# Scores of 27 tiles of the last batch are computed in the first 28 steps and kept in DRAM, and the first batch's last 64 queries become parts of their own

## The chip, the cores and the metric

The kernel runs on one core of one Trainium2 chip. The metric is the device time of one execution in microseconds (us), as the median of several executions; lower is better. A core has a matrix engine (PE, with its weight loads shown as PEld), a vector engine (DVE), an activation engine (ACT), a general engine (POOL), a queue that issues most transfers (SP), and 16 DMA engines that carry them. Each engine takes its instructions in order, and waits on semaphores for the others.

## The reference

Three stages follow each other. The first is attention with only the 32 largest scores of a query kept, the second a gated product over all tokens (here MoE1), the third a routed expert layer with 8 experts (here MoE2).

```
q, k, v: (4, 8, 576, 64)                # batch, heads, sequence, head size
scores = scale * np.matmul(q, k.transpose(0, 1, 3, 2))
kth    = np.partition(scores, -32, axis=-1)[..., -32:-31]
scores = np.where(scores >= kth, scores, -1e9)
x = softmax(scores) @ v                 # as 2304 tokens of 512
x = ((x @ w_a) * (x @ w_b)) @ w_out     # 512 -> 1536 -> 512
idx = argmax over 8 of normalised(x) @ normalised(expert_emb).T / tau
out = gate * (relu(x @ w1[idx]) @ w2[idx])
```

## The kernel before

Attention works on tiles of 128 queries by 576 keys. A batch has 4 pairs of heads, and a pair has 9 tiles: two heads with four tiles of 128 queries each, and one tail tile that holds the last 64 queries of both heads. With 4 batches that is 144 tiles, and the program is written as 144 steps, one tile each. `SEQ` sets the order of the parts: `0A` is the first half of the queries of batch 0 for all four pairs, `0BT` the second half and the tail. Before, 0BT is one part per pair.

Step n does several things for several tiles. DVE searches tile n (`topk`: four MAX8 and three MATCH_REPLACE8 over 576 values; the ops of two tiles alternate, so a tile's search ends in the next step). PE computes the scores of tile n+2 (`scores`: two halves of 288 keys, each with two float32r matmuls, or four in a tail tile) and ACT copies them out of PSUM into a buffer `s`, of which there are 5. For tile n-2 ACT makes the mask (L397, from DVE's threshold), POOL subtracts it (L400, the last reader of `s`), ACT takes the exponential (L402). For tile n-4 PE transposes the weights (L419). When a part ends, PE multiplies with the values (L460) and POOL splits the result into high and low halves. Before a part's scores, its keys and queries are split on POOL (`split_qk`) and transposed on PE (L307, `turn_qk`).

MoE1 runs in the background of these steps. It has 9 groups of 256 tokens; a group can start when the attention of its tokens is done. `background` is called after each piece of a step (each half of the scores, of the transposes, and so on) with a share of what the step leaves of an assumed PE time (`STEP0` 4.5 us up to step 38, `STEP` 5.4 us later), and it takes matmuls from a generator until this budget is used:

```
debt[0] = min(debt[0] + budget, DEBT) if not final else final
```

`DEBT` is 1.0, so one call issues about 1 us of background matmuls whatever the share is. A group has 288 first matmuls (L683, 256 columns) and 72 second ones (L652, 512 columns). Their weights come from the inputs through a conversion on DVE, ACT, POOL and PE (class `Blocks`: L532 to L552, 36 blocks) in the first 36 steps, and are kept in DRAM (`wab_d`) for later groups, which load them again, 512 KB at a time (L620), into 4 buffers `wab`. The converted `w_out` stays in the on-chip tile `wo`.

After step 144 the rest of MoE1 runs alone, then MoE2. The order on PE, DVE, ACT and POOL is the order of the program; the order of the SP queue is chosen when the program is built, by the times that a model of the chip gives. An instruction that waits in the SP queue holds up all that stand behind it.

Of the kernel before, what the change touches and what calls it, by code (L numbers as in the profile page):

```python
# [26 lines left out]
GN = 256  # L27
SEQ = "0A 0BT 1A 1BT 2A 2BT 3AT 3B"
LAG = 2
# [44 lines left out]
AHEAD_Q = 2  # L74
FG = 100000


# [5 lines left out]
def fused_kernel(  # L83
# [114 lines left out]
    with ExitStack() as ph:  # L198
# [72 lines left out]
        def prep(b, pr, part, n, c0):  # L271
            o = Part()
            o.b, o.pr, o.n, o.c0 = b, pr, n, c0
            o.first = now[0] + AHEAD_L
            o.lead = part == [p for bb, p in order_of_parts if bb == b][0]
            o.tail = "T" in part
            o.M = 256 if "A" in part or "B" in part else 0
            o.N = o.M + 64 * o.tail
            o.c = 2 if "B" in part else 0
            if o.lead:  # L280
                load_k(o, b, pr)
            o.qr = load_q(o)
            o.qs = None
            return o

        def split_qk(o):
# [7 lines left out]
            o.qs = qs  # L294

        def turn_qk(o):
# [5 lines left out]
            o.wt = [None, None]  # L302
            o.sm = wk.tile([P, 8], F32, name="sm", bufs=3)
            o.rc = wk.tile([P, 8], F32, name="rc", bufs=3)

# [180 lines left out]

        wo = mk.tile([P, 2, NF, DM], F32R, name="wo", bufs=1)

        class Blocks:
# [3 lines left out]
            def __init__(self):  # L493
                self.order = [(i, f) for f in range(2) for i in range(2)] + [(2, f) for f in range(EARLY)]
                for f in range(2, NF):
                    self.order += [(0, f), (1, f)] + [(2, f + EARLY - 2)] * (f + EARLY - 2 < NF)
                self.raw, self.tiles, self.begun, self.at, self.going = [], {}, 0, [], []
# [26 lines left out]
            def block(self, k):  # L524
# [16 lines left out]
                if i < 2:  # L541
                    wt = mk.tile([P, 2, KC, P], F32R, name="wab", bufs=WB)
                    self.tiles[i, f] = wt
                    hi, lo = wt[:, 0], wt[:, 1]
                else:
                    hi, lo = (wo[:, a, f].rearrange("p (c j) -> p c j", c=KC) for a in range(2))
                act.activation(hi, x, AF.Copy)
# [76 lines left out]
        def moe1(G):  # L624
# [16 lines left out]
            def second(f, tiles=(0, 1)):  # L641
# [5 lines left out]
                for t in tiles:  # L647
# [3 lines left out]
                    for i, (g, w) in enumerate(((lo, 0), (hi, 1), (hi, 0))):  # L651
                        pe.matmul(  # L652
                            px[t], g[:, ts], wo[:, w, f], start=(f == 0 and i == 0), stop=(f == NF - 1 and i == 2)
                        )
# [136 lines left out]
        debt = [0.0, 0.0]  # L791

        def background(budget, final=False):

            debt[0] = min(debt[0] + budget, DEBT) if not final else final
            while debt[0] > 0 and (todo or (final and routes)):
                used = 1.0
                if todo and todo[0][0] <= now[0]:
                    try:
                        if todo[0][2] is None:  # L800
                            todo[0][2] = moe1(todo[0][1])
                        used = next(todo[0][2])
                        if used is None:
                            return
                    except StopIteration:
                        todo.pop(0)
                        continue
                elif not routes:
# [55 lines left out]
        for step in range(-AHEAD_L, NRW + TL + 5):  # L864
            now[0] = step
            if step + AHEAD_L < NRW:
                b, pr, part, first, last, kind, c, slot = rows[step + AHEAD_L]
                if first:
                    with tc.high_priority(offset=FG):
                        o = made[b, pr, part] = prep(b, pr, part, len(made), c0)  # L870
                        coming.append(o)
                    if pr == NP - 1:
                        c0 += o.N
            if 0 <= step + AHEAD_P < NRW:
                b, pr, part, first, last, kind, c, slot = rows[step + AHEAD_P]
                o = made[b, pr, part]
                if first:
                    o.flip = turn_qk(o)
                    flips.append(o)
                    parts.append(o)  # L880
# [52 lines left out]
            tg = turn(live[i]) if 0 <= i < NRW else none  # L933
            sg = scores(live[step + AHEAD_Q]) if 0 <= step + AHEAD_Q < NRW else none
            mg = mixes[0] if mixes else none
            cost, n = 0.0, 0
# [372 lines left out]
```

## Time and profile before

| | |
|---|---|
| Median of 3 executions | 1334.83 us (1330.85 to 1334.86) |
| The profiled execution | 1327.13 us, of which the span of its instructions is 1325.2 us |
| Busy in the span | PE 1181.8 us (89%), DVE 920.5 (69%), ACT 820.3 (62%), POOL 715.1 (54%) |
| Attention, start of first and last search | 18.0 us and 874.9 us |
| Written and read in DRAM | 40.85 MB and 195.38 MB |

Busy shares over the whole span say little here, since the stages differ: in attention DVE is busiest, after it PE. A row of PE matmuls gives their modelled durations, which overlap; how fast they follow each other is read from the starts of successive rows in the timeline. "Idle before us <-releasers" is the time an engine stood idle right before such instructions, and what ended it.

### The profile page before, as it was taken

To read this page: it belongs to the slowest core of one execution; us is meant where nothing else is said; L and a number is where in the kernel's file an instruction comes from. 1 tells how busy PE (TensorE), PEld (TensorE's weight loads), DVE (VectorE), ACT (ScalarE), POOL (GpSimd) and SP (SyncE) were. 2 spreads that over 40 slices of the span, in tenths; PEclk is the share of its full clock that TensorE was granted. 3 is DMA by queue.
4 is the path that set the end of the run, shared out by engine and by line. 5 is a ranking of instruction groups with operands and counts; after the bars stand their busy time and mean duration, and the time that the engine had idled before them with its cause. 6 is when DMAs were issued, how large, how long until landed. Compare 5 with 4: busy or idle time off the path is not lost. (4 is left out here: it accounts for less than half of the span.)

```text
span 1325.2 us, 23082 instructions
## 1 busy us (share of the span) xinstructions
PE 1181.8 (89%) x7828; PEld 992.9 (75%) x7829; DVE 920.5 (69%) x1991; ACT 820.3 (62%) x1953; POOL 715.1 (54%) x1160
## 2 busy tenths in 40 slices
PE   4767878987999998999999998799999989999996
PEld 3444756666888787887887787678898868888885
DVE  6989999987899988998889899750100135444440
ACT  4776888876777777776778776663532335444441
POOL 4555767755676777765767766564455321111100
PEclk9786999897999999998999999799999999999999
DMA  6333476454666666665666656457998145555520
GB/s 210 121 103 124 143 244 210 177 179 146 182 184 223 185 208 193 212 180 176 204 183 192 202 165 203 146 170 247 331 300 246 40 129 197 174 168 173 176 91 19
DMA packets 125707, 237.00 MB, mean 179 GB/s; under 512 B 22765, under 2 KB 71021, under 8 KB 125586
## 3 DMA queue, kind: packets, MB, share of 16 engines
q1 hardware_dynamic: 121426, 225.20, 53.8%
q0 software_dynamic: 4160, 10.29, 2.4%
q8 instruction: 63, 1.03, 0.3%
q14 instruction: 58, 0.48, 0.1%
HBM read 195.38 MB, written 40.85 MB: 178 GB/s over the span
## 5 line engine op out<-in xcount | busy, mean ns | idle before, releaser
L385 DVE MAX8 t<-y 128x8 f32<-128x576 f32 x432 | 312.0, 750 | 3.1
L400 POOL TENSOR_TENSOR z<-s,z 128x576 f32<-128x576 f32 x144 | 206.2, 1432 | 105.6 <-ACT z L397 103.4
L683 PE MATMUL ab<-xg,wab 128*128 128x256 f32 x1440 | 215.8, 292 | 5.6 <-ACT gab L687 3.8
L388 DVE MATCH_REPLACE8 y<-t,y 128x576 f32<-128x576 f32 x288 | 214.0, 743 | 0.0
L683 PEld LDWEIGHTS ab<-xg,wab 128*128 128x128 f32 x1440 | 190.5, 193 | 9.0 <-ACT gab L687 4.4
L683 PE MATMUL ab<-raw,wab 128*128 128x256 f32 x1152 | 173.6, 292 | 6.8 <-ACT gab L687 4.4
L419 PE MATMUL tr<-ident,z 128*128 128x128 f32 x720 | 136.0, 289 | 44.5 <-ACT z L402 36.1
L402 ACT ACTIVATE z<-z,bi 128x576 f32<-128x576 f32 x144 | 111.6, 775 | 79.5 <-POOL z L400 79.4
L683 PEld LDWEIGHTS ab<-raw,wab 128*128 128x128 f32 x1152 | 152.4, 193 | 10.8 <-ACT gab L687 5.7
L385 DVE MAX8 t<-s 128x8 f32<-128x576 f32 x144 | 107.7, 748 | 54.1 <-ACT s L365 48.8
L364 PE MATMUL tr<-kT,qT 128*128 128x288 f32 x512 | 127.8, 334 | 18.1 <-ACT s L365 13.9
L422 ACT ACTIVATE wt<-tr 128x384 f32<-128x384 f32 (+2 forms) x320 | 127.4, 413 | 17.7 <-PE tr L419 16.9
L365 ACT ACTIVATE s<-tr 128x288 f32<-128x288 f32 x288 | 118.9, 413 | 30.0 <-PE tr L364 28.6
L419 PEld LDWEIGHTS tr<-ident,z 128*128 128x128 f32 x720 | 91.6, 147 | 60.2 <-ACT z L402 39.7
L652 PE MATMUL x<-wo,gh 128*128 128x512 f32 x432 | 135.6, 395 | 0.0
L1015 DVE TENSOR_TENSOR u<-raw,u 128x1024 fp32r<-128x1024 f32 x64 | 76.2, 1221 | 83.5 <-ACT u L1014 60.6
L1064 POOL DMA_INDIRECT out_dram<-o,ids x24 | 24.0, 1000 | 200.4 <-ACT o L1063 197.1
L1092 PE MATMUL y<-u,hT 128*128 128x512 f32 (+1 forms) x528 | 128.0, 396 | 0.4 <-DVE hT L1197 0.4
L639 POOL TENSOR_TENSOR gab<-gab 128x256 f32<-128x256 f32 x108 | 81.9, 758 | 84.7 <-ACT gab L687 79.5
L364 PEld LDWEIGHTS tr<-kT,qT 128*128 128x128 f32 x512 | 89.1, 205 | 32.1 <-ACT s L365 17.5
L397 ACT ACTIVATE z<-s,bi 128x576 f32<-128x576 f32 x144 | 112.7, 783 | 0.0
L1092 PEld LDWEIGHTS y<-u,hT 128*128 128x128 f32 (+1 forms) x528 | 89.7, 173 | 27.6 <-DVE hT L1197 0.5
(178 smaller groups left out, 2211.8 us busy)
## 6 DMA issues: line engine op xcount, KB each, us to landing
wab<-wab_d SPq DMA_DIRECT2D x192, 512.0 KB
raw<-in_moe_w_dram SPq DMA_DIRECT2D x28, 1024.0 KB
wab_d<-wab SPq DMA_DIRECT2D x24, 512.0 KB
kT_d<-kT SPq DMA_DIRECT2D x16, 576.0 KB
kT<-kT_d SPq DMA_DIRECT2D x16, 576.0 KB
vs<-in_v_dram SPq DMA_DIRECT2D x32, 256.0 KB
raw<-in_moe_w_a_dram SPq DMA_DIRECT2D x12, 512.0 KB
raw<-in_moe_w_b_dram SPq DMA_DIRECT2D x12, 512.0 KB
```

The lines of the kernel that those rows point to most:

```text
L364: pe.matmul(p, l, r, start=(i == 0), stop=(i == len(terms) - 1))
L365: act.activation(t.s[:, cs], p, AF.Copy, scale=SCALE)
L385: dve.max(v, cur)
L388: dve.match_replace(out=rest, in_to_replace=v, in_values=cur, imm_value=LOWEST)
L397: act.activation(t.w, t.s, AF.Relu, bias=t.bi[:, 1:2], scale=-HUGE)
L400: pool.tensor_tensor(t.w, t.s, t.w, op=OP.subtract)
L402: act.activation(t.w, t.w, AF.Exp, bias=t.bi[:, 0:1], accum_out=t.o.sm[:, t.slot : t.slot + 1])
L419: pe.transpose(pt[:, i * P : (i + 1) * P], t.w[:, k0 : k0 + P], ident)
L422: act.activation(th[:, sl, w], pv[:, :, src], AF.Copy)
L652: pe.matmul(px[t], g[:, ts], wo[:, w, f], start=(f == 0 and i == 0), stop=(f == NF - 1 and i == 2))
L683: pe.matmul(p[:, i], wt[:, a, c, :], xg[x][:, c, :], start=(j == 0), stop=(j == len(terms) - 1))
L1092: pe.matmul(p[:m], (hi, lo)[a], u[:, b, f % 4, :], start=(f == 0 and i == 0), stop=(f == NF2 - 1 and i == 2))
```

## The change

Three things change together. First, `SEQ` becomes `0A 0B 1A 0T 1BT ...`: the four tail tiles of batch 0 are no longer in the steps 16 to 35 but are four parts of one tile each, in steps 48 to 51. Second, a generator `early` is put into the background: in the first 28 steps it loads queries and keys of batch 3, pairs 0 to 2, transposes them, and computes the scores of their 27 tiles with plain float32 matmuls (one per half tile; two heads at a time, each on 64 of the 128 rows). ACT copies them out, and 27 DMAs store them in `pre_d`. It works in the memory of the last five blocks of `wo`, which become a tile `woz` of their own. In the place of those tiles `scores` now issues one load from `pre_d` into `s`, and these parts no longer load, split or transpose queries and keys. Third, the conversion takes the blocks of `w_out` two places later (`SH`).

```diff
-SEQ = "0A 0BT 1A 1BT 2A 2BT 3AT 3B"
+SEQ = "0A 0B 1A 0T 1BT 2A 2BT 3AT 3B"
...
+PRE = [(3, pr) for pr in range(3)]
+PW0 = 3.0
+F7 = 7
+SH = 2
...
+    pre_d = drm.tile([len(PRE) * 9, P, S], F32, name="pre_d")
...
+            o.pre = PRE.index((b, pr)) if (b, pr) in PRE else None
+            if o.pre is not None:
+                return o
             if o.lead:
                 load_k(o, b, pr)
             o.qr = load_q(o)
...
         def scores(t):
             o = t.o
             t.s = wk.tile([P, S], F32, name="s", bufs=SB)
+            if o.pre is not None:
+                sp.dma_start(t.s, pre_d[9 * o.pre + (8 if t.kind == 2 else 4 * t.kind + o.c + t.c)])
+                return
...
+        def early():
+
+            a = mk.tile([P, 2, NF - F7, DM], F32, name="woz", bufs=1)
...
+            def load(b, pr):
+                h0 = 2 * pr
+                for x, src in ((kr, k), (qr, q)):
+                    for h in range(2):
+                        sp.dma_start(x[:, 0:4, h], src[b, h0 + h, 0:512, :].rearrange("(p c) d -> p c d", c=4))
+                    sp.dma_start(x[0:64, 4], src[b, h0 : h0 + 2, 512:576, :].rearrange("h s d -> s h d"))
...
+            for i in range(len(PRE)):
+                for x, to in ((kr, kT), (qr, qT)):
+                    pt = bank()
+                    for c in range(4):
+                        flip(pt, c * P, x[:, c])
+                    act.activation(to[:, 0:512], pt, AF.Copy)
+                    yield 0.43
...
+                for c in range(5):
+                    for j in range(2):
+                        cs = slice(j * 288, (j + 1) * 288)
+                        to = [(h, st[2 * (c % 2) + h]) for h in range(2 if c < 4 else 1)]
+                        pts = [bank()[:, :288] for _ in to]
+                        for h, _ in to:
+                            hs = slice(h * 64, (h + 1) * 64)
+                            if c < 4:
+                                pe.matmul(pts[h], qT[hs, c * P : (c + 1) * P], kT[hs, cs], start=True, stop=True)
+                            else:
+                                pe.matmul(pts[h], qm, kT[:, cs], start=True, stop=True)
+                        for h, s_ in to:
+                            act.activation(s_[:, cs], pts[h], AF.Copy, scale=SCALE)
+                            if j:
+                                sp.dma_start(pre_d[9 * i + (4 * h + c if c < 4 else 8)], s_)
+                        yield 0.75 if c < 4 else 0.5
...
-            while debt[0] > 0 and (todo or (final and routes)):
+            while debt[0] > 0 and (todo or left[0] or (final and routes)):
...
+                elif left[0]:
+                    used = further()
+                    if used is None:
                         continue
...
+            if sg is not none and live[step + AHEAD_Q].o.pre is not None:
+                for _ in sg:
+                    pass
+                sg = none
```

Three places show how the order on the engines moves. The first is PE in the first steps, around the scores of tiles 5 to 7. Before, it reads (L307 transposes keys and queries, L364 makes scores, L419 transposes weights, L550 and L551 belong to the conversion):

```order
L550 MATMUL tr<-x1T,ident 128x512
L551 MATMUL tr<-wab,minusr 128x512
L364 MATMUL tr<-kT,qT 128x288 x2
L307 MATMUL tr<-identr,ks 128x128 x8
L419 MATMUL tr<-ident,z 128x128 x3
L364 MATMUL tr<-kT,qT 128x288 x2
L419 MATMUL tr<-ident,z 128x128 x2
```

The same place of the change reads (L632, L633, L378, L318, L433 are the same lines under new numbers, L560 is the new matmul):

```order
L632 MATMUL tr<-x1T,ident 128x512
L633 MATMUL tr<-wab,minusr 128x512
L378 MATMUL tr<-kT,qT 128x288 x2
L318 MATMUL tr<-identr,ks 128x128 x4
L560 MATMUL ab<-woz 128x288 x2
L318 MATMUL tr<-identr,ks 128x128 x4
L433 MATMUL tr<-ident,z 128x128 x3
L378 MATMUL tr<-kT,qT 128x288 x2
L433 MATMUL tr<-ident,z 128x128 x2
L560 MATMUL ab<-woz 128x288 x2
```

Pairs of new matmuls stand between the old ones, one or two pairs in a step; in the whole program there are 30 such places, with 54 matmuls. The second place is PE in steps 113 and 114, around the transposes of tiles 109 and 110. Before (`x` is MoE1's second product, `qm` the queries of a tail tile; `xg` its input):

```order
L419 MATMUL tr<-ident,z 128x128 x3
L364 MATMUL tr<-kT,qm_115 128x288 x4
L419 MATMUL tr<-ident,z 128x128 x2
L364 MATMUL tr<-kT,qm_115 128x288 x4
L307 MATMUL tr<-identr,qs 128x128 x2
L307 MATMUL tr<-identr,ks 128x128 x4
L652 MATMUL x_8289<-wo,gl 128x512
L652 MATMUL x_8289<-wo,gh 128x512 x2
L419 MATMUL tr<-ident,z 128x128 x3
```

The change, from the same transposes on (L765 is MoE1's first product, L683 before):

```order
L433 MATMUL tr<-ident,z 128x128 x3
L765 MATMUL ab<-xg_8180,wab 128x256 x4
L433 MATMUL tr<-ident,z 128x128 x2
L765 MATMUL ab<-xg_8182,wab 128x256 x4
L433 MATMUL tr<-ident,z 128x128 x3
L765 MATMUL ab<-xg_8180,wab 128x256 x8
L734 MATMUL x_8696<-woz,gl 128x512
```

The scores and the transposes of keys and queries are gone, and the background work does not grow in their place. Counted over the program, 1912 of the 2592 first matmuls of MoE1 stand ahead of the transposes of the last tile before, and 1900 now. The third place is the SP queue at the loads of tiles 112 to 114; before, it has no such loads, and its rows there are:

```order
L620 DMA wab_8620<-wab_d_62 128x1024
L620 DMA wab_8622<-wab_d_62 128x1024
L334 DMA kT_d_63<-kT_8480 128x1152
L620 DMA wab_8712<-wab_d_62 128x1024
L620 DMA wab_8714<-wab_d_62 128x1024
```

In the change (L702 is the load of MoE1's weights, L367 that of a tile's scores, L834 stores routed rows, L267 loads values):

```order
L367 DMA s_9342<-pre_d_66 128x576
L834 DMA row_d_64<-xr_8368 128x516
L702 DMA wab_9515<-wab_d_62 128x1024
L367 DMA s_9413<-pre_d_66 128x576
L702 DMA wab_9517<-wab_d_62 128x1024
L367 DMA s_9473<-pre_d_66 128x576
L267 DMA vs_9645<-in_v_dram 128x2x256
```

Each load of scores stands behind a load of weights, which waits until PE has used up the buffer that it fills. By the order on PE, that point lies in step n-2 for 15 of the 27 tiles n, which is the step in which the scores of tile n were made before, and in an earlier step for the other 12.

## Rows read from the trace of the kernel before

**Rows 1.** The page: busy tenths of an engine in 40 slices of 33 us.

```profile
PE   4767878987999998999999998799999989999996
DVE  6989999987899988998889899750100135444440
PEclk9786999897999999998999999799999999999999
```

**Rows 2.** Windows by stage: length, then busy us (instructions) of PE, PEld, DVE, ACT, POOL; clock; DMA.

```profile
18.00:165.00 147.00, 106.63 (x555) 76.15 (x554) 138.38 (x299) 108.89 (x253) 85.47 (x109) 0.80 0.42 137
165.00:263.00 98.00, 83.12 (x500) 59.61 (x500) 97.70 (x195) 81.17 (x186) 72.67 (x83) 0.97 0.61 211
263.00:485.00 222.00, 204.58 (x1499) 175.02 (x1498) 196.17 (x449) 161.04 (x416) 149.63 (x252) 0.96 0.61 184
485.00:647.00 162.00, 151.82 (x1128) 130.09 (x1127) 143.75 (x329) 118.50 (x306) 111.73 (x197) 0.97 0.64 196
647.00:885.00 238.00, 215.71 (x1606) 183.90 (x1607) 207.83 (x474) 170.24 (x444) 160.83 (x284) 0.97 0.61 183
885.00:1325.00 440.00, 415.66 (x2528) 364.06 (x2524) 130.44 (x224) 175.79 (x345) 130.45 (x226) 0.99 0.53 175
```

**Rows 3.** Groups of 647 to 885 us: busy us, mean ns, idle before and its releasers.

```profile
L385 DVE MAX8 t<-y 128x8 f32<-128x576 f32 x121 | 87.6, 751 | 1.0
L385 DVE MAX8 t<-s 128x8 f32<-128x576 f32 x40 | 30.0, 751 | 22.8 <-ACT s L365 21.2 <-POOL xsb L472 1.4
L737 DVE MAX8 m<-lg 128x8 f32<-128x8 f32 x4 | 0.7, 166 | 5.2 <-ACT lg L733 5.2
L365 ACT ACTIVATE s<-tr 128x288 f32<-128x288 f32 x78 | 32.3, 414 | 10.0 <-PE tr L364 9.9
```

**Rows 4.** Groups of 18 to 165 us, the first steps.

```profile
L550 PE MATMUL tr<-x1T,ident 128*128 128x512 f32 x32 | 24.5, 861 | 1.8 <-POOL x1T L539 1.8
L365 ACT ACTIVATE s<-tr 128x288 f32<-128x288 f32 x51 | 20.9, 413 | 1.7 <-PE tr L364 1.0
L385 DVE MAX8 t<-s 128x8 f32<-128x576 f32 x24 | 17.8, 742 | 1.3 <-ACT s L365 1.3
```

**Rows 5.** Timeline of PE from 262 us: start, us, then the instructions.

```profile
263.15 0.45 PE L307 MATMUL tr<-identr,qs 128*128 128x128 f32 x4
263.44 0.71 PE L683 MATMUL ab<-xg,wab 128*128 128x256 f32 x4
...
265.71 0.43 PE L364 MATMUL tr<-kT,qT 128*128 128x288 f32 x2
265.98 1.10 PE L683 MATMUL ab<-xg,wab 128*128 128x256 f32 x8
...
267.06 1.67 PE L683 MATMUL ab<-xg,wab 128*128 128x256 f32 x12
268.56 1.02 PE L550 MATMUL tr<-x1T,ident 128*128 128x512 f32 x2
```

**Rows 6.** Waits of 647 to 885 us, the SP queue: us in total, times, longest.

```profile
SPq L620 <- PE ab L683: 41.3, 22, 4.0
SPq L620 <- PE tr L419: 33.3, 11, 9.2
SPq L620 <- PE tr L364: 22.5, 13, 3.2
```

**Rows 7.** Timeline of the start, SP, ACT and POOL.

```profile
5.56 0.60 SPq L246 DMA_DIRECT2D kr<-in_k_dram  x1
6.21 4.02 SPq L228 DMA_DIRECT2D qr<-in_q_dram  x4
10.18 1.28 ACT L255 ACT_TABLE_LOAD   x1 [10.05 <-DMA kr<-in_k_dram]
11.32 0.40 POOL L218 TENSOR_SCALAR qs<-qr 128x256 fp32r<-128x256 f32 x1 [9.74 <-DMA qr<-in_q_dram]
```

**Rows 8.** Timeline: the copy of tile 10's second half, and its search.

```profile
67.24 0.42 ACT L365 ACTIVATE s<-tr 128x288 f32<-128x288 f32 x1
76.63 0.74 DVE L385 MAX8 t<-s 128x8 f32<-128x576 f32 x1
```

**Rows 9.** Windows around 830 us, columns as in rows 2.

```profile
831.00:844.00 13.00, 9.40 (x45) 7.00 (x47) 9.06 (x20) 6.81 (x16) 6.01 (x9) 0.50 0.12 40
844.00:860.00 16.00, 13.61 (x111) 12.53 (x110) 12.53 (x33) 11.33 (x30) 8.99 (x16) 0.99 0.64 186
```

**Rows 10.** Waits of 263 to 485 us, DVE for scores.

```profile
DVE t L385 <- ACT s L365: 18.3, 12, 5.1
```

More of the change, by code (lines that the diff above doesn't have):

```diff
@@ L294, in split_qk, with weights @@
             o.qs = qs
+        def weights(o):
+            o.wt = [None, None]
+            o.sm = wk.tile([P, 8], F32, name="sm", bufs=3)
+            o.rc = wk.tile([P, 8], F32, name="rc", bufs=3)
         def turn_qk(o):
@@ L301, in turn_qk @@
                 sp.dma_start(o.kT.bitcast(F32).rearrange("p h j -> p (h j)"), kT_d[o.b * NP + o.pr])
-            o.wt = [None, None]
-            o.sm = wk.tile([P, 8], F32, name="sm", bufs=3)
-            o.rc = wk.tile([P, 8], F32, name="rc", bufs=3)
+            weights(o)
             def flip(pt, c, x):
@@ L485, in finish, with wo, bank, flip @@
                 ready[0] = c0 + N
-        wo = mk.tile([P, 2, NF, DM], F32R, name="wo", bufs=1)
+        wos = [mk.tile([P, 2, F7, DM], F32R, name="wo", bufs=1)]
+        def wo(a, f):
+            if f >= F7 and len(wos) == 1:
+                for _ in sooner:
+                    pass
+                wos.append(mk.tile([P, 2, NF - F7, DM], F32R, name="woz", bufs=1))
+            return wos[f >= F7][:, a, f - F7 * (f >= F7)]
+        def early():
+            a = mk.tile([P, 2, NF - F7, DM], F32, name="woz", bufs=1)
+            a = [a[:, i].rearrange("p f d -> p (f d)") for i in range(2)]
+            qr, kr = (a[0][:, i * 640 : (i + 1) * 640].rearrange("p (c h d) -> p c h d", h=2, d=D) for i in range(2))
+            kT, qT, qm = a[0][:, 1280:1856], a[0][:, 1856:2368], a[0][:, 2368:2496]
+            st = [a[1][:, i * S : (i + 1) * S] for i in range(4)]
+            def load(b, pr):
[4 more added lines that the diff above has]
+                    sp.dma_start(x[0:64, 4], src[b, h0 : h0 + 2, 512:576, :].rearrange("h s d -> s h d"))
+            def bank():
+                return mp.tile([P, 512], F32, name="ab", bufs=2)
+            def flip(pt, at, x):
+                n = x.shape[0]
+                pe.transpose(pt[:, at : at + n], x.rearrange("p h d -> p (h d)"), ident[:n, :n])
+            pool.memset(qm, 0.0)
+            load(*PRE[0])
+            yield 0.0
+            for i in range(len(PRE)):
[5 more added lines that the diff above has]
+                    yield 0.43
+                pt = bank()
+                flip(pt, 0, qr[0:64, 4])
+                flip(pt, P, kr[0:64, 4])
+                act.activation(kT[:, 512:576], pt[:, P : P + 64], AF.Copy)
+                for h in range(2):
+                    hs = slice(h * 64, (h + 1) * 64)
+                    act.activation(qm[hs, hs], pt[hs, 0:64], AF.Copy)
+                if i + 1 < len(PRE):
+                    load(*PRE[i + 1])
+                yield 0.3
+                for c in range(5):
[4 more added lines that the diff above has]
+                        for h, _ in to:
+                            hs = slice(h * 64, (h + 1) * 64)
+                            if c < 4:
[7 more added lines that the diff above has]
+                        yield 0.75 if c < 4 else 0.5
@@ L545, in block @@
                 else:
-                    hi, lo = (wo[:, a, f].rearrange("p (c j) -> p c j", c=KC) for a in range(2))
+                    hi, lo = (wo(a, f).rearrange("p (c j) -> p c j", c=KC) for a in range(2))
                 act.activation(hi, x, AF.Copy)
@@ L652, in second @@
                         pe.matmul(
-                            px[t], g[:, ts], wo[:, w, f], start=(f == 0 and i == 0), stop=(f == NF - 1 and i == 2)
+                            px[t], g[:, ts], wo(w, f), start=(f == 0 and i == 0), stop=(f == NF - 1 and i == 2)
                         )
@@ L791, in fused_kernel, with further @@
         debt = [0.0, 0.0]
+        left = [True]
+        def further():
+            used = next(sooner, None)
+            left[0] = used is not None
+            return used and used * PW0
         def background(budget, final=False):
             debt[0] = min(debt[0] + budget, DEBT) if not final else final
-            while debt[0] > 0 and (todo or (final and routes)):
+            while debt[0] > 0 and (todo or left[0] or (final and routes)):
                 used = 1.0
@@ L877, in fused_kernel @@
                 if first:
-                    o.flip = turn_qk(o)
-                    flips.append(o)
+                    if o.pre is None:
+                        o.flip = turn_qk(o)
+                        flips.append(o)
+                    else:
+                        weights(o)
                     parts.append(o)
```

12 lines of the change are left out of this document (9 added, 3 removed).

## The prediction

> **What bounds the kernel now.** I read the busy tenths first, to see stages, then the windows by stage, then in the stage that the change relieves the groups with their idle times, and last the timeline for the prices of single instructions.
>
> The busy tenths show two regimes [rows 1]. Up to about 885 us, the end of attention, DVE stands at 8 or 9 tenths; after it DVE falls to 4 and PE stays at 9. So the rest of MoE1 and all of MoE2 are bound by PE, and attention mostly by DVE's search. PE has room in the first slices alone, and its clock is partly at the lower level there.
>
> The windows make this finer [rows 2]. From 18 to 263 us DVE is busy 236.1 of 245 us, PE 189.8. Here DVE is the limit, and PE and ACT (190.1 us) are cover. From 263 to 885 us DVE is busy 547.8 of 622 us, and PE 572.1. The modelled ends of PE make its share too high, but the waits say the same: from 647 to 885 us DVE stood idle 238.0 - 207.8 = 30.2 us, and of this 21.2 us ended when ACT had copied scores out, which had waited for PE [rows 2, 3]. From 18 to 165 us the same wait was 1.3 us [rows 4]. So late in attention the search waits for scores that PE brings late, in sums of tens of us and no more: DVE's own 207.8 us is a floor that the change doesn't touch. That the order leaves MoE1's progress at the end of attention where it was is decisive: PE work taken out of attention isn't replaced by MoE1 work, so nothing gets shorter after 885 us. All gain has to come from DVE's idle time before it.
>
> **The change, part by part.** I start from the profiled execution: 1327.1 us, a span of 1325.2 and 1.9 around it. It is 7.7 us under the median of the runs shown, 1334.8; I add the sum to the median.
>
> *Late tiles lose their scores.* For 24 plain tiles 4 matmuls go, for 3 tail tiles 8, so 120. From a start to the next a pair takes 0.27 us [rows 5], so 120 x 0.135 = 16.2 us. For each of the three pairs 27 transposes of keys and queries go, 81 at 0.29 / 4 = 0.07 us [rows 5]: 5.9 us. PE loses 22 us of work from about 650 us on, ACT 54 copies and POOL the splits, which have cover. What it is worth is read from DVE: at most the idle 30.2 us. I keep the 5.2 us that DVE waits in the routing, so the upper bound is 25. Of the 40 searches in this stretch 27 get loaded scores; the other 13 include 9 of the last batch that still wait for PE. I leave 9/40 of the 21.2 us to them, 4.8 us, and take 16.4 us as gone. Of the other 9 us idle I take half, 4.5 us, since PE is late less often. That is -20.9 us.
>
> *The loads take the place of that wait.* Each of the 27 tiles is now 288 KB through the SP queue, with nothing hidden behind it but the lead over DVE. The queue waits for the POOL subtraction that frees `s`, and for the load of weights ahead. The 46 waits of those loads here sum to 97.1 us, 2.1 us each, with one of 9.2 us [rows 6]; behind a load of scores stand loads of weights, which PE waits for next. No row shows this transfer. The nearest are loads at the start: from the last issue of keys to its use 4.6 us, from the end of the last issue of queries to its use 1.1 us [rows 7]. Against this stands the lead. Where DVE is the limit, a tile's scores lay ready 9 us before its search (67.66 to 76.63 us) [rows 8]; by the order, SP is free for the load of tile n at the latest in the step in which its scores were made, so a load of 4.6 us, even behind one load of weights, arrives in time. Where PE is late, DVE is later by one load, but only once, since PE goes on. So the wait per load is between 0 and 2.1 us. I take 0.15 us, one load in ten late by 1.5 us, near the lower end because the lead of 9 us is the row of this same place: 27 x 0.15 = 4 us. Together with the part above -16.9 us.
>
> The Trainium skill ("DMA: Bandwidth & Descriptors", the section on the anatomy of a DMA) gives a fixed cost of about 2.0 us and then bytes by 436 GB/s, fitted on the path of the general engine; for 295 KB that is an estimate of 2.7 us, under my 4.6 us. No run here shows this transfer yet. By it no load would be late, and the sum would lie 4 us lower.
>
> *The tail tiles of batch 0.* Four tiles move from the stretch where PE is cover to steps 48 to 51, where it isn't: each 8 score matmuls of 0.135 us, 2 transposes, and a product with the values and normalisation that are now an issue of their own, some 2 us a tile, 8 us in all as an upper bound. Against it groups 1 and 2 may start 4 steps earlier. At step 40 the order now has 328 first matmuls done and had 292; 36 at 1.5 / 12 = 0.125 us [rows 5] is 4.5 us of PE work that goes into steps where PE had nothing in the background. At step 76 both stand alike (868 and 864), so it comes back only if DVE waits less in between: it waited 18.3 us for scores from 263 to 485 us [rows 10]. I take 0, with -4.5 and +8 as bounds.
>
> *The first 28 steps.* 30 places with 54 new matmuls. L550 is a plain float32 matmul of 512 columns, 861 ns at a mean clock of 0.80 [rows 2, 4]; 288 columns are 0.48 us. If both heads run side by side it is 30 x 0.48 = 14.5 us, if not 26; with transposes, under 35 us, and 54 copies of 413 ns [rows 4] and 21 for the transposed operands are under 31 us on ACT. Cover: from 18 to 165 us PE has 40 us idle, ACT 38 [rows 2], and scores lie ready 9 us ahead [rows 8]. In steps 2 to 4 that lead isn't built up yet; I take +1 us, bounds 0 and +6. The memory `woz` is given to the conversion when the last three stores have landed, one wait in this bound. DVE gets no work here, and POOL one memset.
>
> *Left over.* 12 more first matmuls after attention: 12 x 0.125 = +1.5 us.
>
> Sum: -20.9 + 4.0 + 0 + 1.0 + 1.5 = -14.4 us, so 1312.7 us for an execution like the profiled one and 1334.8 - 14.4 = **1320 us** as median. Its own range, with the bounds of the parts (late idle -25, tails -4.5 to +8, start to +6), is 1308 to 1331.
>
> **The rivals.**
>
> *More.* DVE's idle time from 647 us falls to the routing's 5.2 us, and the tails win their 4.5: -25 - 4.5 + 2.5 = -27, 1308 us. For it: POOL and ACT are relieved too. Against it: stretches with PE far behind recur wherever a group of MoE1 begins.
>
> *Cancelled.* The wait for scores turns into a wait for loads of 0.68 us a tile: -20.9 + 2.5 + 27 x 0.68 = 0, 1335 us. For it: the SP queue's 2.1 us waits, and loads of weights that share the DMA engines. Against it: the lead of 9 us.
>
> *Slower.* One mechanism, the SP queue: half of the loads meet a mean wait of 2.1 us for a `wab` buffer when DVE is already waiting, 1.05 us a tile: -18.4 + 28.4 = +10, 1345 us; with all of them +38. It decides from 0.68 us a tile on. Against it: the wait and the use are both set by PE's place, so it can't be paid again in every step while PE runs on.
>
> *The clock.* Late in attention PE now has 22 us less to do in a stretch that DVE sets, so it idles more. From 831 to 844 us, where it had stood with little to do, its clock was 0.50, the 1.2 GHz level, and 0.99 right after [rows 9]. Such a stretch costs half of its 9.4 busy us, 4.7. Two of them when PE is needed: 1330 us. The skill ("TensorE: Matmul & The Clock Gate", the section on HAM oscillation) states that gaps between groups of matmuls drop the clock to half again and again; the trace agrees at this one place. Against it, PE is still over 85% busy there by the windows less 22 us.
>
> **How the numbers follow.** Chances: forecast 0.48, more 0.14, clock 0.05, cancelled 0.18, slower 0.15. A change under 0.3%, 4 us, can't be told from none here. Faster takes the forecast, more and the clock less a small part: 0.66. Same: 0.19, slower 0.15. The range that leaves out no more than 2 in 10 goes from a little under the larger gain to most of the slower case's half price: 1303 to 1340.
>
> **What would show it.** Right: from about 650 us to the end of attention the stretch is some 17 us shorter, DVE's wait before MAX8 of `s` there falls from 21 us to under 10, now partly for the DMA out of `pre_d`; the time from the first search to step 38 stays within 6 us; the time from the end of attention to the end stays within 3 us. Wrong: DVE waits for `pre_d` in sum over 18 us, or loads of scores are issued right after long waits of L702; or ACT copies of L564 hold up the first steps; or the clock shows 0.5 between 650 us and the end of attention more often than before.

## The result

The change made the kernel slower: 1342.0 us in the median of 8 runs, 1328.3 us before, also of 8; ratio 1.0104, 95% interval 1.0075 to 1.0133. The forecast was 1320 us, and the range ended at 1340. That forecast stood on a median of 1334.8 us, of three executions; taken as a difference it was -14.4 us, and +13.7 was measured. The profiled execution is the slowest of the 8, 1350.9 us: its stages differ from those of before by 24 us in sum, the medians by 13.7. So a few us in a stage can belong to this one execution.

The page of the changed kernel, busy tenths in 40 slices of 34 us:

```profile
PE   5766797888999998799999799889999989999996
DVE  6778797898879988699999999960200135444440
PEclk9697798899899999799999899899999999999999
```

The windows by stage, columns as in [rows 2]; the borders are the same steps as there:

```profile
17.00:185.00 168.00, 126.43 (x662) 83.10 (x660) 135.39 (x300) 127.51 (x308) 85.64 (x111) 0.84 0.53 174
185.00:295.00 110.00, 92.70 (x535) 66.08 (x536) 94.54 (x194) 85.08 (x191) 75.22 (x87) 0.92 0.58 198
295.00:523.00 228.00, 212.28 (x1610) 184.44 (x1609) 196.76 (x452) 163.13 (x435) 154.51 (x276) 0.96 0.66 199
523.00:688.00 165.00, 150.17 (x1095) 127.29 (x1094) 143.75 (x329) 116.32 (x305) 108.16 (x193) 0.95 0.62 184
688.00:903.00 215.00, 192.88 (x1400) 161.32 (x1398) 206.21 (x474) 141.76 (x365) 147.44 (x260) 0.96 0.70 215
903.00:1349.00 446.00, 418.37 (x2532) 366.27 (x2528) 131.13 (x224) 174.52 (x342) 131.54 (x228) 0.99 0.53 173
```

The last row of attention is 23 us shorter than before (215 for 238), with DVE busy 206 us: hardly any idle time is left. But the first two rows, 147 and 98 us before, are 168 and 110. In the first, PE has 20 us more of busy time, ACT 19, DVE 3 less, and yet the idle time of PE (42 us) and ACT (40) is what it was (40 and 38). The new work did not go into the idle time; the stretch grew by about as much, 21 us.

The waits of the changed kernel from 17 to 185 us (us in total, times, longest):

```profile
POOL z L414 <- ACT z L411: 47.1, 20, 6.6
PEld tr L433 <- ACT z L416: 37.7, 16, 3.7
PE tr L433 <- ACT z L416: 33.6, 16, 3.4
DVE rc L444 <- POOL rc L442: 27.6, 4, 9.6
```

DVE doesn't wait for scores there. It waits 27.6 us, in four pieces, at L444, the reciprocal of a part's sums of exponentials, three steps behind the part's last search; before, the same row (L430) had 8.1 us. So the tiles in front of the search are ready, and what lags is the softmax behind it. The starts of the searches say the same: from one to the next, the four gaps with such a reciprocal (behind searches 5, 9, 13 and 17) took 14.8, 12.7, 11.4 and 15.0 us, before 6.8, 9.3, 6.2 and 7.7. That is 24 us more, all that the first 20 steps lost. One such place on DVE's timeline (start, us, instructions, idle before):

```profile
48.01 0.74 DVE L402 MATCH_REPLACE8 y<-t,y 128x576 f32<-128x576 f32 x1
58.39 0.18 DVE L444 RECIPROCAL rc<-rc 128x4 f32<-128x4 f32 x1 [9.64 <-POOL rc L442]
```

PE in the same time:

```profile
50.40 0.90 PE L433 MATMUL tr<-ident,z 128*128 128x128 f32 x3 [2.06 <-ACT z L416]
50.96 0.83 PE L378 MATMUL tr<-kT,qT 128*128 128x288 f32 x2
51.72 1.33 PE L560 MATMUL ab<-woz 64*128 64x288 f32 x4
52.98 0.69 PE L433 MATMUL tr<-ident,z 128*128 128x128 f32 x2
...
55.02 0.80 PE L633 MATMUL tr<-wab,minusr 128*128 128x512 f32 x1
55.62 0.68 PE L378 MATMUL tr<-kT,qT 128*128 128x288 f32 x2
```

And ACT:

```profile
51.34 0.49 ACT L436 ACTIVATE wt<-tr 128x384 f32<-128x384 f32 x1 [0.99 <-PE tr L433]
51.88 0.41 ACT L379 ACTIVATE s<-tr 128x288 f32<-128x288 f32 x1
53.08 0.71 ACT L564 ACTIVATE woz<-ab 128x288 f32<-128x288 f32 x2 [0.79 <-PE ab L560]
53.68 0.78 ACT L411 ACTIVATE z<-s,bi 128x576 f32<-128x576 f32 x1
...
55.85 0.60 ACT L634 ACTIVATE wab<-tr 128x512 fp32r<-128x512 f32 x1 [0.61 <-PE tr L633]
56.35 0.40 ACT L379 ACTIVATE s<-tr 128x288 f32<-128x288 f32 x1
...
57.17 0.77 ACT L416 ACTIVATE z<-z,bi 128x576 f32<-128x576 f32 x1
...
58.67 0.49 ACT L436 ACTIVATE wt<-tr 128x384 f32<-128x384 f32 x1 [0.64 <-PE tr L433]
```

This is a ring: two engines of which each waits in turn for the other. PE opens a step at L433 and stands until ACT has done an exponential, L416. ACT, which keeps its order, reaches the next L416 only behind copies (L379, L634) of what PE makes later in that step. From one first copy of weights to the next, 51.34 to 58.67 us, the ring takes 7.3 us; a search takes DVE 5.09.

Late in attention, 688 to 903 us, DVE and then SP:

```profile
DVE t L399 <- ACT s L379: 3.8, 2, 2.0
...
SPq L367 <- POOL z L414: 25.5, 12, 6.1
```

The wait for scores was 21.2 us [rows 3], and no row has DVE waiting for a load. SP does wait, with a load of scores at the head of its queue, but hardly anybody pays for it: all other engines together wait 0.9 us for these loads. They land in (us, min/median/max):

```profile
DMA to landing us min/median/max: 2.7/3.3/4.5
```

### The profile page after: what moved, and what is told of

Its sections match the earlier page's. It is cut to its first block, busy times and chain, and to the rows that moved or that the text cites. A ratio compares the mean times of both kernels' runs of the same rounds, so it can differ in the third digit from the quotient of the medians.

```text
span 1349.2 us, 23272 instructions
## 1 busy us (share of the span) xinstructions
PE 1197.3 (89%) x7845; PEld 992.7 (74%) x7846; DVE 914.0 (68%) x1995; ACT 813.1 (60%) x1949; POOL 706.3 (52%) x1165
## 5 line engine op out<-in xcount | busy, mean ns | idle before, releaser
L765 PE MATMUL ab<-xg,wab 128*128 128x256 f32 x1440 | 212.4, 290 | 5.4 <-DMA xg<-xl_d 2.3
L765 PEld LDWEIGHTS ab<-xg,wab 128*128 128x128 f32 x1440 | 188.4, 192 | 10.0 <-issue 3.2
L765 PE MATMUL ab<-raw,wab 128*128 128x256 f32 x1152 | 177.4, 296 | 9.2 <-DMA wab<-wab_d 4.8
L433 PE MATMUL tr<-ident,z 128*128 128x128 f32 x720 | 137.3, 292 | 48.2 <-ACT z L416 44.2
L416 ACT ACTIVATE z<-z,bi 128x576 f32<-128x576 f32 x144 | 111.6, 775 | 99.2 <-POOL z L414 99.0
L765 PEld LDWEIGHTS ab<-raw,wab 128*128 128x128 f32 x1152 | 155.2, 197 | 14.3 <-ACT gab L769 6.8
L433 PEld LDWEIGHTS tr<-ident,z 128*128 128x128 f32 x720 | 91.6, 148 | 69.4 <-ACT z L416 50.0
L1195 PE MATMUL y<-u,hT 128*128 128x512 f32 (+1 forms) x528 | 128.1, 396 | 0.3 <-DVE hT L1300 0.3
L378 PE MATMUL tr<-kT,qT 128*128 128x288 f32 x416 | 104.5, 335 | 18.1 <-ACT qT L352 10.8
L379 ACT ACTIVATE s<-tr 128x288 f32<-128x288 f32 x234 | 96.9, 415 | 25.4 <-PE tr L378 23.4
L1195 PEld LDWEIGHTS y<-u,hT 128*128 128x128 f32 (+1 forms) x528 | 89.7, 174 | 27.6 <-DVE hT L1300 0.5
L721 POOL TENSOR_TENSOR gl<-gab,gh 128x256 fp32r<-128x256 f32 x108 | 80.9, 749 | 51.5 <-ACT gh L721 42.6
L402 DVE MATCH_REPLACE8 y<-t,s 128x576 f32<-128x576 f32 x144 | 107.0, 743 | 0.0
```

The source lines that it names most:

```text
L402: dve.match_replace(out=rest, in_to_replace=v, in_values=cur, imm_value=LOWEST)
L416: act.activation(t.w, t.w, AF.Exp, bias=t.bi[:, 0:1], accum_out=t.o.sm[:, t.slot : t.slot + 1])
L433: pe.transpose(pt[:, i * P : (i + 1) * P], t.w[:, k0 : k0 + P], ident)
L721: pend.pop(0)[1]()
L765: pe.matmul(p[:, i], wt[:, a, c, :], xg[x][:, c, :], start=(j == 0), stop=(j == len(terms) - 1))
L1195: pe.matmul(p[:m], (hi, lo)[a], u[:, b, f % 4, :], start=(f == 0 and i == 0), stop=(f == NF2 - 1 and i == 2))
```

## The experiments

Stages below go from the start of one search to that of another, which is the row "MAX8 t<-s" of DVE; in the changed kernel for steps 0, 20, 38, 104 and 143:

```profile
16.85 0.76 DVE L399 MAX8 t<-s 128x8 f32<-128x576 f32 x1 [1.34 <-ACT s L379]
159.96 0.74 DVE L399 MAX8 t<-s 128x8 f32<-128x576 f32 x1
295.08 0.74 DVE L399 MAX8 t<-s 128x8 f32<-128x576 f32 x1
688.25 0.76 DVE L399 MAX8 t<-s 128x8 f32<-128x576 f32 x1 [1.96 <-ACT s L379]
893.22 0.74 DVE L399 MAX8 t<-s 128x8 f32<-128x576 f32 x1
```

The same for every kernel, us of one profiled execution each, with the ratio of its median to that of the kernel before on the same chip:

| kernel | 0-20 | 20-38 | 38-104 | 104-143 | ratio | 95% interval |
|---|---|---|---|---|---|---|
| before | 119.7 | 125.3 | 384.1 | 227.9 | | |
| the change | 143.1 | 135.1 | 393.2 | 205.0 | 1.0104 | 1.0075 to 1.0133 |
| e1 order only | 117.5 | 127.3 | 385.1 | 227.3 | 1.0014 | 1.0001 to 1.0026 |
| e2 early, unused | 143.1 | 133.0 | 389.4 | 228.2 | 1.0272 | 1.0244 to 1.0300 |
| e3 half the copies | 143.1 | 131.0 | 389.7 | 204.2 | 1.0088 | 1.0058 to 1.0117 |
| e4 half the matmuls | 137.7 | 134.1 | 389.4 | 204.3 | 1.0053 | 1.0033 to 1.0074 |
| e5 lag of four | 132.4 | 128.1 | 397.5 | 206.9 | 1.0112 | 1.0086 to 1.0139 |
| e6 order only, lag of four | 119.0 | 129.8 | 388.8 | 227.6 | 1.0099 | 1.0073 to 1.0125 |
| e7 half of both | 131.5 | 131.2 | 389.3 | 204.3 | 1.0003 | 0.9982 to 1.0024 |
| e8 transfers only | 125.8 | 126.4 | 392.7 | 203.7 | 0.9896 | 0.9873 to 0.9919 |
| e9 scores first | 132.9 | 131.2 | 389.7 | 204.9 | 1.0006 | 0.9982 to 1.0031 |
| e10 before, scores first | 115.0 | 124.5 | 383.9 | 227.8 | 0.9977 | 0.9954 to 1.0001 |
| e11 two pairs | 140.8 | 126.9 | 384.5 | 212.7 | 1.0035 | 1.0016 to 1.0055 |
| e12 two pairs, scores first | 130.9 | 126.2 | 383.8 | 211.3 | 0.9986 | 0.9966 to 1.0006 |
| e13 e12 from step 5 | 125.3 | 129.2 | 383.2 | 212.7 | 0.9958 | 0.9937 to 0.9979 |
| e14 three pairs from step 5 | 125.8 | 130.3 | 385.3 | 203.7 | 0.9916 | 0.9887 to 0.9945 |
| e15 the change from step 5 | 135.8 | 158.5 | 394.5 | 203.8 | 1.0233 | 1.0201 to 1.0265 |

The letters in the texts put on record ahead of each run are theories of what costs the time: A the copies on ACT, P the matmuls on PE, S the stores in SP's queue, D and C the plain amount of work. R means the reorder of the tails in e1 and e2, and the ring of PE and ACT from e5 on.

**e1, the order alone.**

```diff
-        sooner = early()
+        sooner = iter(())
...
-            o.pre = PRE.index((b, pr)) if (b, pr) in PRE else None
+            o.pre = None
```

> The new order of parts and the split second matrix stay, but no score is computed ahead and the late tiles compute theirs as before. The trace of the change lost 32 us by the search of step 38 (295.1 us from the start, 263.0 before) and won 23 us from step 104 to step 143. Theory A (the copies on ACT, L564): without them step 38 comes again at 263 +- 6 us, and with the late gain gone too the whole is within 8 us of the kernel before, ratio 0.996 to 1.006. Theory P (the plain float32 matmuls L560) and theory S (stores L566 that stand in SP's queue ahead of loads of weights) expect the same. Rival R (the reorder of the 64-query parts, not the early scores, costs the 32 us): step 38 stays at 285 us or later and the ratio is 1.02 or more.

Step 38 came at 262.8 us, and the ratio is 1.0014. The reorder of the tails costs next to nothing; R in this sense falls.

**e2, computed ahead, not used.** Only the second of the two edits.

> All scores are computed ahead and stored, but nobody loads them: the late tiles compute theirs as before. Theories A, P and S: the loss stays and the late gain goes, so the time is that of the change plus about 23 us, 1360 to 1370 us, ratio 1.022 to 1.032, and 26 to 32 us over the order alone. Rival R: within 6 us of the order alone.

1363.6 us, 34.9 us over the order alone (1328.7) in the same session, a little over what was expected. So the loss belongs to the early scores, and the late gain (228.2 against 205.0 us) to their use.

**e3, half of the copies.**

```diff
+            pool.memset(a[1], 0.0)
...
-                            act.activation(s_[:, cs], pts[h], AF.Copy, scale=SCALE)
                             if j:
+                                act.activation(s_[:, cs], pts[h], AF.Copy, scale=SCALE)
```

> Leaves out the ACT copy L564 of each tile's first 288 keys, 27 of 54; matmuls, stores and loads stay, and the late tiles get zeros there. Theory A: 27 x 0.41 = 11 us less up to step 38, so step 38 at about 284 us and the whole near 1331 us, ratio 1.002. Theory P: ACT's copies have cover, under 3 us less, ratio 1.008 to 1.011. Theory S: stores wait a little less, 2 to 5 us less.

The first 20 steps took 143.1 us, as in the change. Theory A, the copies by themselves, falls.

**e4, half of the matmuls.**

```diff
-                        pts = [bank()[:, :288] for _ in to]
-                        for h, _ in to:
+                        pts = [s_[:, :288] if j else bank()[:, :288] for _, s_ in to]
+                        for h, _ in [] if j else to:
...
-                            act.activation(s_[:, cs], pts[h], AF.Copy, scale=SCALE)
+                            act.activation(s_[:, cs], pts[h], AF.Copy, scale=1.0 if j else SCALE)
```

> Leaves out the matmuls L560 and L562 of each tile's second 288 keys, 27 of 54 scores matmuls; ACT copies the first half from SBUF in their place, so it has as many copies as the change. Late tiles get their first half twice. Theory P: PE's part falls by half of 96 passes and 6 of L562, 54 x 0.25 = 13 us, so step 38 at about 282 us and ratio near 1.000. Theory A: only half of ACT's 7 us of waits for these matmuls goes, 3 to 4 us, ratio 1.006 to 1.010.

137.7 us: 5.4 us less where P wanted 13. Neither engine's work alone is the price.

**e5, e6, a lag of four steps for the transposes.**

```diff
-TL0 = 3
+TL0 = 4
```

> The change, with the transposes of a tile's weights (L433) four steps behind its search from the start (TL0 = 4), where the first 19 steps had three. Halving the copies left the first 20 steps at 143.1 us, halving the matmuls gave 137.7, the order alone 117.5; so theory A falls. Theory R (ring): with a lag of three PE stands each step at L433 until ACT has done the exponential L416 of the same step, and ACT behind it for scores that PE then makes; each early matmul of PE stands on this ring, and PE's idle time there (37 us) can't take it. Then a lag of four takes the wait of PE for L416 from 37 us under 10 and the first 20 steps to 118 to 130 us; ratio 0.992 to 1.001. Rival C (capacity: PE at the lower clock and ACT have too much work whatever the lag): the first 20 steps stay over 138 us, ratio 1.007 to 1.012.

> The order alone without early scores, with the same lag of four. Theory R: the ring took about 6 us a step, little over DVE's search and conversions (110 us busy in 117.5), so 2 to 6 us less, ratio 0.997 to 1.000. Rival C: no change, 1.001.

In e5 the wait of PE at L433 for L416 is gone from the view of waits (33.6 us in the change), with the same work, and the first 20 steps fell by 10.7 us, to 132.4, a little less than the ring theory asked. That speaks for the ring and against capacity. Not all of the idle time went: PE now stands 19.9 us at L632, where it needs a block that POOL converts (L621), and the wait for the reciprocal is still 19.6 us. And the ratio, 1.0112, is the one that the rival expected: steps 38 to 76 took 235.7 us for 227.5. In e6, which has no early work, the lag won nothing (119.0 us, DVE busy 109 of it), its ratio of 1.0099 shows a cost, and the same steps took 226.2 us for 219.1 in e1. So the lag of four costs 7 to 8 us in steps 38 to 76 with early work and without; why is not settled here.

**e7, half of both.**

```diff
+            pool.memset(a[1], 0.0)
...
-                        pts = [bank()[:, :288] for _ in to]
-                        for h, _ in to:
+                        pts = [bank()[:, :288] if j else None for _, s_ in to]
+                        for h, _ in [] if not j else to:
...
-                            act.activation(s_[:, cs], pts[h], AF.Copy, scale=SCALE)
                             if j:
+                                act.activation(s_[:, cs], pts[h], AF.Copy, scale=SCALE)
```

> Leaves out both the matmuls and the ACT copies of each tile's first 288 keys; loads, transposes and stores stay, and late tiles get zeros there. Theory R: PE's part and ACT's part of the ring both shrink, where one alone left the other as long: about half of the 25.6 us, so the first 20 steps at 130 us, ratio 0.999 to 1.004. If the two savings only add (0 and 5.4 us): 137 us.

131.5 us: the two halves give 11.6 us together, where one gave 0 and the other 5.4. So it would be in a ring: what one engine no longer does, the other still holds up.

**e8, the transfers alone.** The transposes of L530 with their copies (L540 to L548) go too; the loads and stores stay.

```diff
+            pool.memset(a[1], 0.0)
...
-                        pts = [bank()[:, :288] for _ in to]
-                        for h, _ in to:
...
-                                pe.matmul(pts[h], qT[hs, c * P : (c + 1) * P], kT[hs, cs], start=True, stop=True)
...
-                            act.activation(s_[:, cs], pts[h], AF.Copy, scale=SCALE)
```

> Leaves out all transposes, matmuls and copies of the early scores; their loads of queries and keys, their 27 stores and the 27 loads stay, and late tiles get zeros. Theory S (the transfers and SP's queue): more than 10 of the 25.6 us stay in the first 20 steps. Theory R: the first 20 steps are back at 116 to 120 us and the late gain of 23 us stays, so 1305 to 1312 us, ratio 0.984 to 0.990.

125.8 us, more than expected, but 8.2 us of it are in steps 2 to 6, 31.9 us for 23.7, and there ACT stood once for a load of another tensor:

```profile
ACT xr L184 <- DMA xr<-in_moe_expert_emb_dram: 8.3, 1, 8.3
```

That load was issued at 42.3 us (10.9 in e1), behind early stores in SP's queue, so it is a price of the transfers; the change has no such wait of ACT. Besides this the transfers cost nothing, and theory S falls as the main cause: it asked for more than 10 us.

**e9, e10, scores first.**

```diff
-            for slot_, g in enumerate((tg, sg, tg, mg, sg)):
+            for slot_, g in enumerate((sg, tg, sg, tg, mg) if step < S1 else (tg, sg, tg, mg, sg)):
```

> The change; in the first 19 steps a step of the order begins with the first half of the next scores, and the transposes of weights L433 come behind it, in turn with the second half. Work and lag stay. Transfers alone cost nothing but one late load in steps 4 to 6; half of PE's and ACT's early work together gave 131.5 us for the first 20 steps, a lag of four 132.4, the whole 143.1. Theory R (ring of PE and ACT): PE has work of its own ahead of its wait for L416, so the ring gets about 1 us a step shorter: first 20 steps at 122 to 135 us, ratio 0.997 to 1.005. Rival C (capacity): first 20 steps over 140 us, ratio 1.009 to 1.013.

> The kernel before with that same edit alone. Its first 20 steps take 119.7 us where DVE is busy 111. Theory R: 112 to 118 us, ratio 0.994 to 0.999. Rival C: no change, 0.999 to 1.001.

132.9 us with the same work, 10.2 less than the change, and the ratio is 1.0006: this edit alone makes the kernel as fast as before. Of the loss up to search 38, 33 us, 19 are still there (264.2 us for 245.0); the late gain makes up for them. In the kernel before it gives 4.7 us in the first 20 steps; its ratio, 0.9977, can't be told from no change.

**e11, e12, two pairs.**

```diff
-PRE = [(3, pr) for pr in range(3)]
+PRE = [(3, pr) for pr in range(2)]
```

e12 has the edit of e9 beside this one.

> The change with two of the three pairs, 18 of 27 tiles, computed ahead. If the cost goes with the work: first 20 steps at 117.5 + 17 = 134.5 us. Steps 28 to 32 took 37.6 us with three pairs and 31.1 with none computed: if that is the wait for the last stores out of woz (the early work ended at 210 us, just ahead of step 28), they come at 31 us here, since the early work ends some 5 steps sooner; if not, at 37 us. From step 104 to 143 between 210 and 212 us, if the gain goes with the tiles (two thirds of 23); 206 if it levels off with DVE's idle time. Ratio 0.999 to 1.005.

> Two pairs and the scores first together, the version that should be fastest by theory R: first 20 steps at 118 to 126 us, ratio 0.988 to 0.998. By rival C as two pairs alone, 0.999 to 1.005.

The late gain goes with the tiles: 14.6 us for 18, 22.3 for 27 (from 227.3). The cost of the first 20 steps hardly does: 140.8 us, 2.3 less than with three pairs, though 92 passes of early matmuls (L560) start there in the change and 64 in e11. Up to search 38 it does: 267.7 us for 244.8 in e1, 22.9 more, where the change takes 33.4 more. Steps 28 to 32 come at 31.1 us, 37.6 in the change: that fits the wait of the conversion for the last stores out of `woz`, which e11 doesn't have. e8 and e14, whose last stores are issued at 65 and 143 us, take 31.1 and 29.8 there. In the change, from 205 to 290 us:

```profile
ACT woz L629 <- DMA pre_d<-woz: 4.0, 1, 4.0
```

In e12, steps 2 to 6 took 35.9 us for 23.7, which kept it from the time expected.

**e13, e14, e15, from step 5.**

```diff
+E0 = 5
...
-            while debt[0] > 0 and (todo or left[0] or (final and routes)):
+            while debt[0] > 0 and (todo or (left[0] and now[0] >= E0) or (final and routes)):
...
-                elif left[0]:
+                elif left[0] and now[0] >= E0:
...
+            if step == E0 - 4:
+                next(sooner)
```

e13 has this, two pairs and scores first; e14 three pairs, scores first and `PW0 = 2.0`; e15 this alone.

> Two pairs and scores first, with the early loads issued at step 1 and nothing else of it before step 5. In the two kernels with scores first, steps 2 to 6 took 36 us where the order alone takes 23.7; PE waited there 3.5 us for early queries, and DVE then stood 10.4 us at the reciprocal of the first part. Theory R with its start: lead is lost there once, since the early transposes stand in PE's queue while their loads are under way, before any tile lies ready; then steps 2 to 6 take 23.7 to 27 us, the first 20 steps 118 to 123 us, and the ratio is 0.987 to 0.994. Rival D (the early work costs the same wherever it stands, as capacity): the first 20 steps stay at 129 us or more, ratio 0.997 to 1.001.

> All three pairs, scores first, start at step 5, and each piece of early work charged at two thirds (PW0 = 2) so that it ends before step 28. Theory R with its start: steps 2 to 6 at 23.7 to 27 us, the first 20 steps at 120 to 130 us, steps 28 to 32 at 31 to 37 us, late gain 23 us whole; ratio 0.985 to 0.996. Rival D: first 20 steps at 135 us or more, ratio over 1.000.

> The change with the later start alone, no scores first, three pairs; what isn't done when the second half of the last matrix wants its memory is done there at once. Theory R with its start: steps 2 to 6 at 24 to 27 us instead of 31.6; but steps 8 to 20 keep their 16 us and what is left falls to steps 24 to 32: first 20 steps at 132 to 137 us, ratio 1.003 to 1.010. Rival D: first 20 steps lose as much later as they win in steps 2 to 6, 141 to 145 us.

Steps 2 to 6 took 24.6, 23.9 and 26.6 us, and rival D falls: the same work costs 11 us less there for being started later (e13 against e12), and the first 20 steps keep half of it (125.3 for 130.9, where 118 to 123 were expected). e14 is faster than both kernels, 1316.4 us, ratio 0.9916 (0.9887 to 0.9945). Its windows (a line more in the code, so its L434 is L433; the first border is 5 us short of step 24):

```profile
17.00:165.00 148.00, 119.57 (x663) 77.71 (x663) 132.72 (x294) 122.88 (x304) 83.01 (x109) 0.93 0.61 198
165.00:273.00 108.00, 89.94 (x540) 64.55 (x538) 95.26 (x199) 87.33 (x193) 78.05 (x90) 0.95 0.62 209
...
658.00:872.00 214.00, 194.22 (x1405) 162.76 (x1404) 206.31 (x474) 143.00 (x368) 148.91 (x265) 0.96 0.70 217
```

And its waits from 17 to 143 us:

```profile
PE tr L434 <- ACT z L417: 20.8, 13, 3.1
DVE rc L445 <- POOL rc L443: 14.5, 4, 5.6
```

Both are less than in the change (33.6 and 27.6 us), with all 27 tiles computed ahead and the late gain whole. e15 won its steps 2 to 6 and lost all at step 28, 40.5 us long: the rest of the early work is done there at once, its stores stand in SP's queue, where they wait 24.2 us for ACT's copies (204 to 250 us), and DVE waits for weights behind them. So its ratio is 1.0233, where 1.010 was the most expected. From 204 to 290 us:

```profile
DVE w64t L615 <- DMA raw<-in_moe_w_a_dram: 32.7, 1, 32.7
```

## Why the prediction was wrong

**The step that failed** is the first 28 steps: "Cover: from 18 to 165 us PE has 40 us idle, ACT 38 [rows 2], and scores lie ready 9 us ahead [rows 8]. In steps 2 to 4 that lead isn't built up yet; I take +1 us, bounds 0 and +6." From search 0 to search 38 the change took 278.2 us, before 245.0: +33. The work was counted about rightly: PE's busy time grew by 20 us in the first row of the windows and by 10 in the second, ACT's by 19 and 4, where under 35 and under 31 were counted. The cover was not there, for two reasons. The idle time was the wait of PE and ACT for each other. The trace of the kernel before shows it, in the list of 18 to 165 us that [rows 4] come from:

```profile
L419 PE MATMUL tr<-ident,z 128*128 128x128 f32 x103 | 24.6, 349 | 36.2 <-ACT z L402 34.2 <-ACT wt L422 1.9
```

The prediction took the 40 us and did not ask what ended them. The waits of the same stretch show both directions:

```profile
PE tr L419 <- ACT z L402: 34.2, 17, 3.4
...
ACT wt L422 <- PE tr L419: 12.4, 16, 1.0
ACT xsb L463 <- PE tr L460: 10.5, 4, 3.5
```

34.2 us of PE's 40 ended when ACT had done an exponential, and in the changed kernel it is 33.6. Work put into this ring made it longer and didn't fill its waits. In the first 20 steps PE was busy 79 us in the order alone, 92 in e7, 95 in e4, 104 in the change and 107 in e3; it stood 39, 39, 43, 39 and 36 us, about the same whatever it had to do. With the work of the change in another order it stood 30 us in e5 and 33 in e9, and these steps took 10 us less. And the lead of 9 us was that of scores before the search; the search was held up from behind, by a reciprocal that stands in DVE's queue ahead of the next search and needs the softmax of tiles already searched.

Of the 33 us, the order within a step is 10 in the first 20 steps (e9). The start at step 5 takes 5 off in steps 2 to 6 (e15, 26.6 for 31.6); with scores first it takes 11 (e13 against e12), but there scores first had itself cost 4 (e9, 35.7). Without the later start PE's queue held early transposes while their loads were under way: PE's longest wait for one was 2.4 us in the change, just ahead of search 2, and 3.5 in e12, just behind it. The memory of `woz` is 6.5 us in steps 28 to 32 (e11), of which 4.0 are seen as a wait. These overlap, so they are not a sum. The three edits of e14 together, all the early work kept, take 22 of the 33 us away (256.1 us to search 38); which wait the other 11 are is not shown.

The prediction's own range, 1308 to 1331, doesn't come out of its bounds either: with 4 us for the loads they give 1311 and 1333. That is not why it failed.

**The late tiles** were right in kind and under-sized: -20.9 and +4.0 for the loads were forecast, -16.9; measured -22.9 from search 104 to 143. The term that was furthest off is the loads: no wait of DVE for them, 0 and not 4. They landed in 2.7 to 4.5 us, inside the 4.6 that the prediction took as a bound. By the Trainium skill ("DMA: Bandwidth & Descriptors", anatomy of a DMA) the estimate for such a load was 2.7 us; the fastest of 27 took that, the median 3.3, so the trace agrees at its lower end only. The rivals "cancelled" and "slower" by the SP queue fall, though SP's waits were as long as feared.

**The tails of batch 0** were right at 0: with the order alone steps 38 to 104 take 385.1 us for 384.1. The 9 us that the change loses there (5 in e2, with the same early work) come another way. Seven kernels whose early work lasts, by the order, up to the conversions at step 28 (the change, e2, e3, e4, e7, e8 and e9) take 223.7 to 227.5 us from step 38 to 76; the five where it ends sooner or is absent (e1, e11 to e14) take 216.9 to 219.3. e15, whose early work lasts as long, takes 230.9. e8 is among the slow ones without any early matmul or copy, so it is not their work; why, is open. e5 and e6 stand apart by the cost of their lag, and before and e10, with another order of parts, take 221.4 and 222.9.

**Left over**: 12 more matmuls behind attention, +1.5 us, can't be told in the traces; of the first products 720 start behind attention (885 and 903 us) in both. The time from there to the end was to stay within 3 us and grew by 6, 440 to 446 us. From the last search to the end the kernels here take 447.8 to 456.0 us in their profiled executions, e1 455.9 without any early work, so one execution can't tell whether the change did that.

**The clock** as a rival late in attention didn't come: 0.96 there, 0.97 before.

## What to carry to other kernels

Idle time of an engine is cover only if what ends it is not the same loop that the new work joins. Ask, for each wait that makes up the idle time, whether the releasing engine in its turn waits for this one: then count the new work in full, or move it first, behind another lag or another place in the step. And a lead in front of the limiting engine says nothing of what it needs from behind: look for the instruction in its queue that waits for the results of its own earlier work.

## What the hardware showed that was not expected

The four passes of an early pair on PE took 1.33 us at 51.72 us in the change and 0.76 us in its next step:

```profile
58.56 0.76 PE L560 MATMUL ab<-woz 64*128 64x288 f32 x4
```

The granted clock was 0.50 from 51.7 to 53.0 us and 1.00 from 58.5 to 59.3: the levels of 1.2 and 2.4 GHz. A longer stretch is a mixture of both: 0.93 from 17 to 165 us in e14; in the change, 0.84 from 17 to 185. It was lower where PE stood 2 us in each step, in the kernel before too (0.80, [rows 2]). The Trainium skill ("TensorE: Matmul & The Clock Gate", HAM oscillation) says that gaps between groups of matmuls bring the clock down again and again, and these rows agree.

How much of the 10 us of e9 is its higher clock (0.88 from 17 to 150 us) and how much the shorter ring, no run here tells apart. But e5 took as much off at the clock of the change (0.82 from 17 to 149 us, for 0.81 from 17 to 160), so a higher clock isn't needed for it. And in e8, without the early matmuls, the clock was lower still (0.72 from 17 to 143 us), and nothing was lost but the one late load.
